# Filling TensorE's planned idle time with matmuls of a constant in an S4 convolution and GEGLU kernel

## The chip, the cores and the metric

The kernel is written for one Trainium2 chip and runs on one core of it. The metric is the device time of one execution in microseconds (us); less is better. A core has a matrix engine (TensorE, PE in the profile, with its weight loads listed as PEld), a vector engine (DVE), a scalar engine (ACT), GpSimd (POOL) and a sync engine (SP) that mostly issues transfers. Each engine works through its own list of instructions in order and waits on semaphores for the others. Matmul results land in PSUM banks.

## What is computed

```python
mod = (_silu(c) @ w_mod).reshape(c.shape[0], 6, 1, -1)
sa, ca, ga, sb, cb, gb = (mod[:, 0], mod[:, 1], mod[:, 2], mod[:, 3], mod[:, 4], mod[:, 5])
h = _layernorm(x, axis=-1) * (1 + ca) + sa
x = x + ga * _A_ref(h, A_A_re, A_A_im, A_B_re, A_B_im, A_C_re, A_C_im, A_log_dt, A_Dskip)
h = _layernorm(x, axis=-1) * (1 + cb) + sb
x = x + gb * _B_ref(h, B_w_gate, B_w_up, B_w_down)
```

x is 2048 tokens by 448 channels. `_A_ref` builds a kernel of 2048 taps for each channel from 256 complex modes, K = Re(sum of C exp(dt A l) dt B), and convolves it with h by FFT. `_B_ref` is (gelu(h w_gate) * (h w_up)) w_down with 1792 inner features.

## The kernel before

The program has two halves. In the first, the S4 half, parameters are turned into exponents and phases (DVE and ACT, function `prep`), written to memory and read back as stationary operands `lt`; TensorE expands them into exponent tables (`exps`, tasks x.mm and y.mm) and phase tables (`angles`); ACT takes exp and sin of them; DVE multiplies (`mults`); TensorE contracts over the modes (`kgen`). Beside it the input is normalised and taken through two stages of a Fourier transform (`u_norm_a`, whose task ua is TensorE's, and `u_stage_b`), then multiplied with the kernel's transform and taken back (`k_fft`, `t_fft`), through memory, into tiles `yi`. The rows of `mod` come from `mod_row`: its task m.mm is four float32 matmuls of silu(c), broadcast as the stationary operand, with 448 columns of w_mod, and its task m.ev is a copy on ACT.

The second half works on four blocks of 512 tokens: `conv_out` ends the inverse transform (task co.mm), adds the residual (DVE), normalises, and transposes on TensorE (co.t in the first block); `gate_up` makes gate and up products in float16 pieces; `down_first` and `down` make the last product.

The order of the work is not written out. Each piece is a task with a cost per engine, dependencies and buffers it takes from pools of fixed size. `Plan.order` simulates the engines with these costs, a due value `v` and tables of leads, picks the next task again and again, and sets `t.start` and `t.end` in its own clock. `Plan.run` then emits the tasks' instructions in that order, and each engine keeps to it on the chip, waiting on semaphores.

Names the text needs: `eps` is a column of 128 rows holding 1e-5 in the tile `small`, set by a memset at L371; `pf`, `pg`, `kg`, `pd` and `pq` are PSUM tiles. Lines: m.mm L768, m.ev L771, ua L832 (its copies out at L408 on ACT and L410 on DVE), y.mm L612, loads of `lt` L575, co.mm L1246 (320 columns) and L1251 (128 columns), the residual add L1257, co.t L1294 and L1296, gate and up L1371 and L1365. In the first block co.mm is split: the first two of its four pieces do the 320 columns (co.mme) and the 128 columns (co.mml) as separate tasks, since the last channels' transform comes back from memory later than the others.

## Time and profile before

| | |
|---|---|
| time, median of 3 runs | 825.76 us (824.82 to 829.9) |
| profiled execution: time | 825.18 us |
| profiled execution: span from first to last instruction | 823.4 us |
| TensorE busy (matmul) | 748.4 us, 91% of the span |
| DVE busy | 599.6 us, 73% |
| ACT busy | 470.3 us, 57% |
| mean granted TensorE clock | 0.969 |

All times of the views are counted from the first instruction of the profiled execution. Its own time is 1.8 us longer than its span. A row of a view gives the start and length, or the busy time, of a group of instructions, its engine and line, the tile written and the tiles read, the shapes, and in square brackets how long the engine had stood idle just before and what ended that. The row PEclk shows the clock that TensorE was granted in tenths of full speed. In the records a float32 matmul appears twice, so a group of four such matmuls is x8.

### The profile page before, as it was taken

What the parts mean: (1) busy time and instruction counts of PE and PEld (TensorE: products, weight loads), DVE (VectorE), ACT (ScalarE), POOL (GpSimd) and SP (SyncE); (2) the same over time, 40 slices, a digit from 0 to 9 for tenths busy, and PEclk for the clock granted to TensorE, in tenths of its full rate; (3) what the DMA queues carried; (4) which work ended last, traced back from release to release, by engine and by line L of the source; (5) the groups of instructions that cost most, each with busy time, mean ns of one, the idle gap of its engine ahead of it and who ended that gap; (6) DMA issues with size and microseconds to landing.
All of it is one profiled execution on the core that took longest, in us unless ns stands there. A gap on an engine that the chain in (4) does not pass through costs nothing.

```text
span 823.4 us, 19059 instructions
## 1 busy us (share of the span) xinstructions
PE 748.4 (91%) x8166; PEld 461.2 (56%) x8166; DVE 599.6 (73%) x981; ACT 470.3 (57%) x629; POOL 6.0 (1%) x14
## 2 busy tenths in 40 slices
PE   2786789999799999998589999999999999999997
PEld 1344344444577767778466445444496445864477
DVE  7789998999889989897494783178863686244542
ACT  5598999899968999971244553034442353113320
POOL 0000000000000000000200000000000000000000
PEclk9888799999999999999889999999999999999999
DMA  9552369996858846899669756245315322022101
GB/s 283 148 167 92 105 189 236 285 273 200 236 146 257 233 133 193 253 307 295 189 197 298 267 179 179 75 140 166 117 53 146 135 91 90 34 79 90 45 12 35
DMA packets 92526, 136.83 MB, mean 166 GB/s; under 512 B 21280, under 2 KB 75200, under 8 KB 92442
## 3 DMA queue, kind: packets, MB, share of 16 engines
q1 hardware_dynamic: 89514, 133.75, 53.8%
q10 hardware_dynamic: 2608, 1.61, 0.8%
q8 instruction: 64, 1.05, 0.5%
q0 software_dynamic: 320, 0.26, 0.1%
q14 instruction: 20, 0.16, 0.1%
HBM read 100.48 MB, written 36.01 MB: 166 GB/s over the span
## 4 chain that ended last, share of the span: by engine, by line
PE 67%; ACT 12%; DVE 10%; DMA 6%; issue 3%; SPq 1%; DVEq 0%; ACTq 0%
PE pq L1371 30%; PE pq L1472 9%; PE pd L1441 3%; PE kg L710 3%; ACT fg L643 2%; PE pg L630 2%; PE pf L999 2%; PE pq L1365 2%; PE pf L768 2%; ACT my L617 2%; PE pf L1085 2%; PE pf L895 2%; DVE tx L679 2%; DMA fg<-in_w_mod 2%; PE pd L1472 1%
## 5 line engine op out<-in xcount | busy, mean ns | idle before, releaser
L1371 PE MATMUL pq<-ht,wr 128*128 128x512 f16 (+1 forms) x1200 | 250.0, 367 | 0.0
L1371 PEld LDWEIGHTS <-wr 128*128 128x128 f16 x1200 | 115.4, 98 | 128.6 <-issue 11.0
L1378 ACT ACTIVATE ge<-pq 128x512 f32<-128x512 f32 (+1 forms) x60 | 33.9, 568 | 144.5 <-PE pq L1365 93.9
L1385 DVE TENSOR_TENSOR fq<-ge,pq 128x512 f32<-128x512 f32 (+1 forms) x60 | 38.5, 649 | 72.1 <-PE pq L1371 48.2
L1397 ACT ACTIVATE hh<-fq 128x1024 f16<-128x1024 f32 (+1 forms) x49 | 47.1, 963 | 54.5 <-DVE fq L1385 41.8
L1472 PE MATMUL pq<-d,hh 128*128 128x224 f16 x504 | 73.2, 259 | 0.0
L710 PE MATMUL kg<-ty,tx 128*32 128x64 f32 x3584 | 61.8, 221 | 11.3 <-DVE ty L687 6.4
L679 DVE TENSOR_TENSOR tx<-mx,fg 128x1024 f32<-128x1024 f32 x56 | 68.0, 1220 | 4.0 <-ACT fg L654 2.2
L683 DVE TENSOR_TENSOR ty<-my,fg 128x1024 f32<-128x1024 f32 x56 | 68.2, 1219 | 3.0 <-PE kg L710 2.8
L710 PEld LDWEIGHTS kg<-ty,tx 128*32 128x32 f32 x3584 | 53.0, 110 | 27.6 <-issue 11.2
L1472 PE MATMUL pq<-d,hlo 128*128 128x224 f16 x252 | 65.3, 259 | 0.0
L1400 DVE TENSOR_TENSOR hlo<-fq,hh 128x1024 f16<-128x1024 f32 (+1 forms) x49 | 53.9, 1104 | 5.3 <-ACT hh L1397 5.0
L643 ACT ACTIVATE fg<-pg 128x1024 f32<-128x1024 f32 x56 | 56.6, 1019 | 1.9 <-issue 1.2
L1472 PEld LDWEIGHTS <-hh 128*128 128x128 f16 x588 | 56.7, 98 | 1.1 <-issue 0.4
L617 ACT ACTIVATE my<-pg 128x1024 f32<-128x1024 f32 x56 | 55.3, 1041 | 3.1 <-PE pg L612 2.9
L999 PE MATMUL pf<-q,fc 128*128 128x160 f32 x264 | 42.9, 313 | 0.3 <-DVE q L989 0.3
L630 PEld LDWEIGHTS <-lt 64*128 64x128 bf16 x336 | 20.7, 95 | 37.4 <-issue 20.7
L999 PEld LDWEIGHTS pf<-q,fc 128*128 128x128 f32 x264 | 37.7, 195 | 6.3 <-issue 3.3
L630 PE MATMUL pg<-ea,lt 64*128 64x512 bf16 x168 | 34.9, 389 | 6.2 <-ACT fg L643 4.4
L687 DVE TENSOR_TENSOR ty<-my,fg 128x512 f32<-128x512 f32 x56 | 38.4, 686 | 0.0
L686 DVE SCALAR_TENSOR_TENSOR ty<-my,fg 128x512 f32<-128x512 f32 x56 | 38.4, 685 | 0.0
L735 PE MATMUL kg<-ak,ke 128*64 128x128 f32 x448 | 32.1, 284 | 6.2 <-DVE ke L730 4.4
(172 smaller groups left out, 1196.3 us busy)
## 6 DMA issues: line engine op xcount, KB each, us to landing
wr<-w_d SPq DMA_DIRECT2D x21, 896.0 KB
fc<-in_k_fc SPq DMA_DIRECT2D x20, 576.0 KB
u_d<-so SPq DMA_DIRECT2D x32, 224.0 KB
w<-in_wgu SPq DMA_DIRECT2D x14, 512.0 KB
ui<-u_d SPq DMA_DIRECT2D x10, 672.0 KB
w_d<-wr SPq DMA_DIRECT2D x7, 896.0 KB
fq<-in_wd SPq DMA_DIRECT2D x14, 448.0 KB
us<-uo SPq DMA_DIRECT2D x22, 240.0 KB
```

The source lines that it names most:

```text
L617: A.activation(yb.tile.rearrange("p a b c -> p (a b c)"), pb.tile, AF.Exp)
L630: T.matmul(pa[:, nh * 512:nh * 512 + 512], w, x, start=(k == 0), stop=(k == 2))
L643: A.activation(fb.tile[:, 0].rearrange("p x (n k) -> p n x k", n=2), pb.tile.rearrange("p (n x k) -> p n x k", n=2, x=2), AF.Sin, scale=TW ...
L679: V.tensor_mul(tx.tile, xb.tile[:, xm, None, :].to_broadcast([128, 2, 512]), fb.tile[:, :, 0])
L683: V.tensor_mul(ty.tile[:, 1], yb.tile, fy()[:, 1, :, None, :].to_broadcast([128, 16, 2, 32]))
L710: T.matmul(kg[32 * g:32 * g + 32, 2 * (s % 2) + q, :64], tx[:, r, nh, 4 * q + g], ty[:, r, nh, 4 * q + g], start=(r == 0 and nh == 0), sto ...
L999: T.matmul(pz.tile[:, e % 32 - sl0], fc.tile[:, i, 1 + t], pp.tile[:, t, i], start=(t == 0 and e != 32), stop=(t == 1 and e != 0))
L1371: T.matmul(pb[k].tile[:, ts], wr.tile[:, 4 * lo + t, k, c0:c0 + 128], ht[:, m, ts], start=f % 2 == 0 and i == 0, stop=f % 2 == 1 and i == 9)
L1385: V.tensor_mul(to if half is None else to[:, half:half + 1], *src)
L1397: A.activation(hg.tile[0][:, cb, c], fq.tile[:, c], AF.Copy)
L1400: V.tensor_sub(hg.tile[1][:, cb, c], fq.tile[:, c], hg.tile[0][:, cb, c])
L1472: T.matmul(bank(k)[:, m], x[:, p, q[0], ts], w[:, p, q[1]], start=new and m == 0 and p == 0 and z == 0, skip_group_check=True, stop=i in ( ...
```

## The change

`Plan.run` now keeps, for tasks on TensorE, how long TensorE stands idle in the planner's own clock ahead of the task (`t.idle`). A new helper `spin` takes the planned idle time less 1.2 us, divides it by 0.4 us for 448 columns (less for narrower ones in proportion), and emits that many matmuls of `eps` with `eps`, both broadcast and float32, into the bank that the task overwrites next. Six kinds of tasks call it: x.mm, kgen, m.mm, ua, co.mm and co.t. The order of the tasks stays what it was.

```diff
     def run(self):
+        free = 0.0
         for t in self.order():
+            if t.on == "PE":
+                t.idle, free = t.start - free, t.start + t.eng["PE"]
             t.fn(t.on) if len(t.eng) > 1 else t.fn()
...
+    def spin(me, dst, w=D):
+        for _ in range(int(max(0.0, me[0].idle - 1.2) / (0.4 * w / D))):
+            T.matmul(dst, eps.to_broadcast([128, 128]), eps.to_broadcast([128, w]), start=True, stop=True)
+
...
+        me = []
+
         def mm():
             pb.tile = fft.tile([128, D], FT, name="pf")
+            spin(me, pb.tile)
             for t in range(4):
...
         t2 = add("m.mm", {"PE": 3.22}, v, mm, [t1, t_si], [pb], [wb])
+        me.append(t2)
...
                 for h in range(2):
                     pbs[h].tile = fft.tile([128, D], FT, name="pf")
+                spin(me, pbs[0].tile)
                 for h in range(2):
...
                     if i == 0:
                         pb.tile = POOLS["pd"].tile([128, D], FT, name="pd")
+                    spin(me, pb.tile[:, c0:c1], c1 - c0)
...
                 pt.tile = POOLS["ps"].tile([128, 4, 128], FT, name="pq")
+                spin(me, pt.tile.rearrange("p k t -> p (k t)")[:, :D])
                 for k in range(3):
```

In x.mm the call stands behind `pb.tile = gen.tile(...)`, in kgen behind the allocation of `kg`; both read like the ones shown.

In the built program the helper gives instructions at four places, 105 matmuls in all, and all are on TensorE: 33 ahead of the first m.mm, 7 ahead of the first ua, 59 of 128 columns ahead of the first co.mml, and 6 ahead of the third co.t. No other engine's list has other instructions than before. In the changed program line numbers are larger: L768 is L784, L832 is L852, L612 is L623, L1246 and L1251 are L1270 and L1275, L1294 and L1296 are L1322 and L1324; the helper's matmul is L417.

TensorE's list at the start of the program, with the semaphores that each row waits for (`fg` holds w_mod, `pk` silu(c), `xt` the normalised input). Before:

```order
L768 MATMUL pf<-fg,pk 128x448 [waits DMAHW6_49,DMAHW1_49,Activation_49]
L768 MATMUL pf<-fg,pk 128x448 x3
L768 MATMUL pf<-fg,pk 128x448 [waits DMAHW7_49]
L768 MATMUL pf<-fg,pk 128x448 x3
L768 MATMUL pf<-fg,pk 128x448 [waits DMAHW0_49,Activation_49]
L768 MATMUL pf<-fg,pk 128x448 x3
L832 MATMUL pf<-xt,au 128x448 [waits DMAHW4_49,DMAHW5_49,DVE_49,Activation_49]
L832 MATMUL pf<-xt,au 128x448 [waits Activation_49]
```

The same place now:

```order
L417 MATMUL pf<-small 128x448 [waits DVE_49]
L417 MATMUL pf<-small 128x448 x32
L784 MATMUL pf<-fg,pk 128x448 [waits DMAHW6_49,DMAHW1_49,Activation_49]
L784 MATMUL pf<-fg,pk 128x448 x3
L784 MATMUL pf<-fg,pk 128x448 [waits DMAHW7_49]
L784 MATMUL pf<-fg,pk 128x448 x3
L784 MATMUL pf<-fg,pk 128x448 [waits DMAHW0_49,Activation_49]
L784 MATMUL pf<-fg,pk 128x448 x3
L417 MATMUL pf<-small 128x448 [waits Activation_49]
L417 MATMUL pf<-small 128x448 x6
L852 MATMUL pf<-xt,au 128x448 [waits DMAHW5_49,DMAHW4_49,DVE_49]
L852 MATMUL pf<-xt,au 128x448 [waits Activation_49]
```

The 33 matmuls wait for DVE alone (the memset of `eps`), and the loads' semaphores are waited for behind them; the 7 take over a wait for an ACT copy that frees their bank.

TensorE's list at the passage from the first half to the second (`yi` is the transform read back, `ai` and `ident` are constants, `xn` is the normalised block). Before:

```order
L1246 MATMUL pd<-yi,ai 64x320 x4
L1251 MATMUL pd<-yi,ai 64x128 x4
L1246 MATMUL pd<-yi,ai 64x320 x2
L1251 MATMUL pd<-yi,ai 64x128 x2
L1246 MATMUL pd<-yi,ai 64x320 x2
L1251 MATMUL pd<-yi,ai 64x128 x2
L1294 MATMUL pq<-ident,xn 128x128 x3
L1296 MATMUL pq<-ident,xn 64x128 x2
L1294 MATMUL pq<-ident,xn 128x128 x3
L1296 MATMUL pq<-ident,xn 64x128 x2
L1294 MATMUL pq<-ident,xn 128x128 x3
L1296 MATMUL pq<-ident,xn 64x128 x2
```

The same place now:

```order
L1270 MATMUL pd<-yi,ai 64x320 x4
L417 MATMUL pd<-small 128x128 x59
L1275 MATMUL pd<-yi,ai 64x128 x4
L1270 MATMUL pd<-yi,ai 64x320 x2
L1275 MATMUL pd<-yi,ai 64x128 x2
L1270 MATMUL pd<-yi,ai 64x320 x2
L1275 MATMUL pd<-yi,ai 64x128 x2
L1322 MATMUL pq<-ident,xn 128x128 x3
L1324 MATMUL pq<-ident,xn 64x128 x2
L1322 MATMUL pq<-ident,xn 128x128 x3
L1324 MATMUL pq<-ident,xn 64x128 x2
L417 MATMUL pq<-small 128x448 x6
```

The 59 stand ahead of the matmuls that read the late part of `yi`, and take over from them a wait for DVE (the residual add that reads the same bank); the 6 stand ahead of the third transpose, and wait for nothing.

## The prediction

> **What bounds the kernel now.** I read the page first, for the shape of the run.

> ```profile
> span 823.4 us, 19059 instructions
> PE   2786789999799999998589999999999999999997
> PEclk9888799999999999999889999999999999999999
> ```

> Each digit is a fortieth of the span, 20.6 us. TensorE is short of work and of clock at the start and around 400 us, and nearly full from there on. The change puts matmuls at just these two places, so I followed the chain of waits through them; first the start.

> ```profile
> 2.63 13.19 DMA fg<-in_w_mod
> 15.96 12.27 PE pf L768 x24
> 28.33 4.86 DMA lt<-lh_d
> 33.24 1.39 PE pg L612 x4
> ...
> 45.44 5.77 DMA xt<-in_A_u
> ```

> The chain runs through m.mm without a gap: a load until 15.82, the twelve matmuls until 28.23, then the load of `lt` and what needs it. Why the load of `lt` hangs on m.mm is seen in ACT's own list, in order of time, where it stands behind the copies of m.mm's results:

> ```profile
> 22.24 0.54 ACT L771 ACTIVATE rows<-pf 128x448 f32<-128x448 f32 x1 [6.01 <-PE pf L768]
> ...
> 28.25 0.54 ACT L771 ACTIVATE gs<-pf 128x448 f32<-128x448 f32 x1 [1.84 <-PE pf L768]
> 28.33 1.38 ACTq L575 DMA_DIRECT2D lt<-lh_d  x2
> ```

> So whatever moves the end of m.mm moves the first half. Now the same chain at the passage to the second half:

> ```profile
> 376.54 4.73 PE pf L1069 x40
> ...
> 389.63 8.95 PE pf L1085 x80
> ...
> 407.64 2.45 DMA yi<-y
> ...
> 410.23 0.91 PE pd L1251 x4
> ...
> 419.50 0.70 DVE xn L1289
> ...
> 420.25 0.94 PE pq L1294 x6
> 421.18 0.43 PE pq L1296 x4
> 421.61 3.85 PE pq L1371 x20
> 425.46 0.32 PE pq L1365 x4
> 425.78 2.29 PE pq L1371 x20
> ```

> A readback of `yi` ends at 410.09, a little TensorE follows, then DVE's residual adds and norms until 420.20, the third transpose, and the gate and up products, which keep TensorE full to the end. Its L1371 rows are the same twenty matmuls, 3.85 us in one and 2.29 in the other.

> **The price of one added matmul.** The planner's idle time is divided by 0.4 us for 448 columns. The trace has no such matmul; the nearest is m.mm's: float32, a broadcast stationary operand, 448 columns moving. Four of them late in the run, and then those of L768 at the start in two stretches (length, TensorE busy, records, weight loads, granted clock, DMA):

> ```profile
> 233.23 3.01 PE pf L768 x8
> ```

> ```profile
> 20.50:22.00 1.50, 1.50 (x3) 0.68 (x2) 1.00 0.42 163
> 22.00:23.50 1.50, 1.50 (x5) 0.76 (x4) 1.00 0.30 93
> ```

> Late in the run a matmul takes 0.752 us (3.01 for four, two records each). At the start they run at half that pace until about 22 us: the clock column reads 1.00 in both rows, but the count of records per 1.5 us says otherwise, and I go by the count. So TensorE needed 6.0 us of work (15.96 to 22) to get its clock. The other stretches of that kind, with the granted clock in the last column but two:

> ```profile
> 33.20:36.60 3.40, 3.36 (x11) 1.59 (x11) 2.10 (x5) 3.25 (x5) 0.00 (x0) 0.50 0.04 16
> ...
> 410.50:413.90 3.40, 3.40 (x20) 2.08 (x20) 2.57 (x9) 0.59 (x2) 0.00 (x0) 0.50 0.95 260
> 413.90:417.50 3.60, 3.28 (x26) 2.12 (x22) 3.46 (x9) 1.20 (x3) 0.00 (x0) 0.91 0.90 356
> 417.50:421.20 3.70, 0.95 (x8) 0.83 (x10) 3.62 (x8) 3.54 (x6) 0.00 (x0) 1.00 0.00 1
> 421.20:424.00 2.80, 2.80 (x16) 1.88 (x17) 2.73 (x6) 1.04 (x1) 0.00 (x0) 0.53 0.51 161
> 424.00:427.00 3.00, 3.00 (x26) 2.17 (x25) 2.96 (x6) 1.29 (x2) 0.00 (x0) 0.87 0.34 139
> ```

> After the wait for `yi` the clock is at half from 410.2 to about 414.5 (0.91 over 3.6 us is 0.65 us at half), 4.3 us; it falls again after the 0.95 busy us of 417.5 to 421.2 and is back at about 424.8 (0.87 over 3.0 us is 0.8 at half), 3.6 us.

> **The start, 33 matmuls.** They wait only for the memset of `eps`:

> ```profile
> 0.81 0.06 DVE L371 MEMSET small<- 128x1 f32 x1 [0.81 <-PEq L1632]
> ```

> They start at about 1.0. 33 x 0.752 is 24.8 us. While the clock is still at half they lose half of that stretch; of stretches between 3.6 and 6.0 us that is 1.8 to 3.0, and I take 2.5. They end at 28.3. m.mm's data landed at 15.82, but m.mm stands behind them in TensorE's list. It then has the full clock, 12 x 0.752 = 9.0 us, and ends at 37.3 where it ended at 28.23: **+9.1 us** (8.4 to 9.6). The gain of the clock, 12.27 - 9.0 = 3.3 us, is in this. Nothing covers the delay: behind the copies of L771 stand, in ACT's list, a store of `lh` and the loads of `lt`, and DVE's norms need the copies. SP's loads are not held by it, but none of them ends the chain here.

> [...]

> **The start, 7 matmuls.** They fill the gap ahead of the first ua, and ACT waited for TensorE a little later:

> ```profile
> 31.48 1.16 PE L832 MATMUL pf<-xt,au 64*128 64x448 f32 x4 [3.26 <-issue]
> ```

> ```profile
> 39.28 3.77 ACT L617 ACTIVATE my<-pg 128x1024 f32<-128x1024 f32 x4 [1.68 <-PE pg L612]
> ```

> 7 x 0.752 = 5.3 us in a gap of 3.26: ua comes 2.0 us later. Behind ua stands y.mm, whose `lt` lands 5.0 us after m.mm (33.24 - 28.23); it now waits for 5.3 and a ua of 0.6, +0.9. In exchange TensorE has its full clock where it had 0.50, and ACT's wait of 1.68 us can go. From 39.28 on ACT is full and TensorE's clock no longer matters. Bounds -1.7 and +2.0; I take **0**, as the two ends weigh about the same.

> **The passage, 59 matmuls of 128 columns.** What waits and for how long, on TensorE, and the add that they wait for, on DVE:

> ```profile
> 398.94 1.30 PE L1246 MATMUL pd<-yi,ai 128*64 128x320 f32 x8
> 410.23 1.32 PE L1251 MATMUL pd<-yi,ai 128*64 128x128 f32 x8 [9.99 <-DMA yi<-y]
> ```

> ```profile
> 399.75 0.49 DVE L1257 TENSOR_TENSOR x<-x,pd 128x320 f32<-128x320 f32 x1 [4.15 <-PE pd L1246]
> ```

> Start 400.24. Nearest rows for 128 x 128 x 128 float32: L1085, 8.95/40 = 0.224 us, and L1069, 4.73/20 = 0.2365; from the wide one by columns, 0.752 x 128/448 = 0.215. 59 take 12.7 to 14.0 us; with the row that has most of them, 13.2. They end at 413.4, the data were there at 410.09: **+3.2 us** (2.7 to 3.8). The clock is kept, so the four records of L1251 on the chain take half of 0.91: -0.45.

> **The passage, 6 matmuls.** The gap they fill:

> ```profile
> 420.25 0.94 PE L1294 MATMUL pq<-ident,xn 128*128 128x128 f32 x6 [3.07 <-DVE xn L1289]
> ```

> 6 x 0.752 = 4.5 us in 3.07: **+1.4** (at half clock 9.0, +5.9, which after 13 us of matmuls I don't expect). The first twenty of L1371 keep the clock: 2.29 for 3.85, **-1.6**. TensorE is the chain from there on, so the rest arrives at the end. Passage together +3.2 - 0.45 + 1.4 - 1.6 = **+2.6** (2.1 to 3.2).

> **Sum.** The profiled execution took 825.18 us (span 823.4 and 1.8 around it). 825.18 + 9.1 + 0 + 2.6 = 836.9; it stands 0.6 below the median of 825.76, so I forecast **837 us**; its own range is 834 to 840.5.

> **Rivals.**

> *The delay of the start is hidden.* The chain shows one way only; if another within a few us set the end of the first half (between 45 and 376 us the chain goes from ACT to DVE to transfers), part of the 9.1 would vanish. It decides from 3 us hidden: below 834 the loss is within 1%. All hidden: 825.2 + 2.6 = 828. For it: the 5.77 us load in the chain may get shorter when it runs at another time. Against: that load is released by TensorE, and ACT and DVE both stand behind L771, in lists whose order is fixed. 0.15.

> *Not slower: the added matmul is as cheap as the planner's 0.4 us.* A moving operand that is one broadcast column is in no row. From half of 0.752 downwards the 33 end by 1.0 + 33 x 0.376 + 2.5 = 15.9, when the data land, the 7 take 2.8 of 3.26 us, the 59 take 6.7 of 9.99, and the 6 take 2.4 of 3.07. Then only the gains are left: -3.3 - 1.7 - 0.45 - 1.6 = -7, 818 us, still within 1%. Against: L768 has the same type, width and broadcast weights and never ran faster. 0.07.

> [...] That is inside this rival, with 0.02 of its 0.07; the trace, at 0.376 us a record, disagrees.

> *The constant does not bring up the clock.* If tiny constants did not count as work, the 33 would take 49.6 us and m.mm its 12.27 as before: +34.6; the 7 some +5, the 59 some 4 us at full and the rest at half clock, +12, the 6 +6: 882 us. Against: m.mm's own work raised the clock with broadcast weights. 0.05.

> *My forecast*, 0.73.

> **Range and chances.** 1% of the median, 8.3 us, is about what a measurement of this kernel can tell from no change: 817.5 to 834. My range is 828 to 841: it takes in the hidden start and leaves out the cheap matmul, the cold constant and a tail of 0.06. Slower: forecast 0.73 less 0.05 below 834, cold 0.05 and 0.01 of the hidden start, 0.74. Faster: 0.02 of the cheap one. Same: 0.24.

> **What would show it.** In the profile after: records of the new line at 0.376 us for 448 columns and 0.112 for 128, the first stretch ending near 28 and the first m.mm right behind it with no idle time; the copy of L771 near 32; the first ua near 42.6; 13 us of the new line at the passage, with L1251's successor following it and the wait for `yi` gone; granted clock near 1.00 through both. I am wrong if m.mm starts before 27, if the distance from the end of m.mm to the end of the first half shrinks by 3 us or more, or if the new records are shorter or stay at 0.75 us.

## The result, and the profile after

The changed kernel takes 834.83 us (median of 6 executions, 832.26 to 840.71); the kernel before took 826.12 us beside it (median of 6, 823.47 to 830.65). The ratio is 1.0104, with a 95% interval of 1.0062 to 1.0146: 8.6 us slower, between 5.1 and 12.1. That is slower by just over 1%, where the forecast was 837 us. The profiled execution of the changed kernel took 836.45 us, 11.3 more than that of before (825.18).

The page of the changed kernel, its slices of 20.9 us:

```profile
span 834.6 us, 19477 instructions
PE   9968687999999999998999999999999999999997
PEclk9999598999999999999999999999999999999999
```

TensorE now reads 9 in the first two slices and in the 20th and 21st (they were 2 and 7, 5 and 8), and the clock is 9 in all four. (In the fifth slice the clock reads 5 where it read 7 before.) The whole gets longer all the same. The chain of waits at the start shows why; its columns are the start, the length and what it was:

```profile
0.92 27.52 PE pf L417 x66
28.44 9.02 PE pf L784 x24
37.47 5.29 PE pf L417 x14
42.75 1.00 PE pf L852 x4
...
55.04 5.45 DMA xt<-in_A_u
...
408.24 0.71 PE pd L1270 x4
409.51 13.44 PE pd L417 x118
422.95 0.42 PE pd L1275 x4
...
429.04 4.73 PE pq L417 x12
433.77 0.67 PE pq L1322 x6
434.81 2.29 PE pq L1400 x20
437.42 2.29 PE pq L1400 x20
```

The 33 added matmuls (66 records of line 417) are now the start of the chain, in place of the load that landed at 15.82. They end at 28.44; m.mm (L784, formerly L768) takes 9.02 us where it took 12.27, and ends at 37.46 where it ended at 28.23. At the passage the 59 end at 422.95, where L1275 (formerly L1251) began at 410.23. The 6 take 4.73 us, and gate and up (L1400, formerly L1371) get both their twenties in 2.29. The second of these twenties began at 425.78 before and begins at 437.42 now, 11.64 later; the rest to the end takes as long as before (397.28 us, 397.69 in before).

ACT's list shows the delay handed on as the prediction read it: the copies of m.mm's results late, and the load of `lt` behind the last of them.

```profile
31.49 0.55 ACT L788 ACTIVATE rows<-pf 128x448 f32<-128x448 f32 x1 [15.75 <-PE pf L784]
...
37.58 1.37 ACTq L582 DMA_DIRECT2D lt<-lh_d  x2
```

That load is issued 9.25 us later than before (28.33).

### The profile page after: what moved, and what is told of

Read it like the earlier page. It is cut to its first block, busy times and chain, and to the rows that moved or that the text cites. A ratio compares the mean times of both kernels' runs of the same rounds, so it can differ in the third digit from the quotient of the medians.

```text
span 834.6 us, 19477 instructions
## 1 busy us (share of the span) xinstructions
PE 791.3 (95%) x8376; PEld 488.0 (58%) x8376; DVE 598.9 (72%) x981; ACT 470.3 (56%) x629; POOL 6.0 (1%) x14
## 3 DMA queue, kind: packets, MB, share of 16 engines
q10 hardware_dynamic: 2608, 1.61, 0.7%
## 4 chain that ended last, share of the span: by engine, by line
PE 70%; ACT 13%; DVE 9%; DMA 4%; issue 3%; SPq 1%; ACTq 0%; DVEq 0%
PE pq L1400 29%; PE pq L1501 9%; PE pf L417 4%; PE pd L1470 4%; ACT fg L654 3%; ACT my L628 2%; PE kg L722 2%; PE pq L1394 2%; PE pf L916 2%; ACT fg L646 2%; PE pf L1106 2%; PE pg L641 2%; DVE ty L694 2%; DVE tx L690 2%; PE pd L417 2%
## 5 line engine op out<-in xcount | busy, mean ns | idle before, releaser
L1400 PE MATMUL pq<-ht,wr 128*128 128x512 f16 (+1 forms) x1200 | 248.5, 365 | 0.0
L1400 PEld LDWEIGHTS <-wr 128*128 128x128 f16 x1200 | 114.5, 98 | 127.9 <-issue 11.0
L641 PEld LDWEIGHTS <-lt 64*128 64x128 bf16 x336 | 20.5, 94 | 40.3 <-issue 23.9
L916 PE MATMUL pf<-ui,fu 128*128 128x448 f32 x66 | 33.7, 606 | 1.6 <-DMA ui<-u_d 1.6
```

The lines of the kernel that those rows point to most:

```text
L641: T.matmul(pa[:, nh * 512:nh * 512 + 512], w, x, start=(k == 0), stop=(k == 2))
L916: T.matmul(pb.tile, fu.tile[:, i], ui.tile[:, EORD[e0 + i] % 32 - s0], start=True, stop=True)
L1400: T.matmul(pb[k].tile[:, ts], wr.tile[:, 4 * lo + t, k, c0:c0 + 128], ht[:, m, ts], start=f % 2 == 0 and i == 0, stop=f % 2 == 1 and i == 9)
```

## The experiments

Mine and three rivals stood at the outset. Mine: the parts add up, +9.1 at the start, 0 for the 7 and +2.6 at the passage, since an added matmul costs 0.752 us and every microsecond ahead of m.mm reaches the end. The rivals of the prediction: the start's delay is partly hidden further on, the matmul is cheaper than that, or the constant does not raise the clock. All edits below are against the changed kernel. The kernel before ran beside each group, with medians of 826.59 to 828.26 us; each difference is worked out from the ratio to it.

**The start alone, and the passage alone.** The first keeps only m.mm's 33, the second only the 59 and the 6:

```diff
-                t.idle, free = t.start - free, t.start + t.eng["PE"]
+                t.idle, free = t.start - free if t.n in ("m.mm",) else 0.0, t.start + t.eng["PE"]
...
+                t.idle, free = t.start - free if t.n in ("co.mml", "co.t") else 0.0, t.start + t.eng["PE"]
```

> Only the 33 matmuls ahead of the first m.mm are left in. Theory 'overrun' (each added matmul takes 0.752 us, nothing hides what goes past the arrival of the data): the 33 end near 28.4 us, m.mm ends near 37.4 instead of 28.2, the first matmul of t.fwd starts at 385.7 instead of 376.5, the wait for yi is back at about 10 us, and the time is 9 us above the kernel before. Rival 'hidden' (another way sets the end of the first half): m.mm ends at 37.4 too, but t.fwd starts within 3 us of 376.5 and the time is within 3 us of the kernel before. Rival 'extra load' (the loss of the changed kernel has nothing to do with this place): no change in time.

> Only the 59 and the 6 matmuls at the passage are left in. Overrun: m.mm ends at 28.2 and t.fwd starts at 376.5 as in the kernel before; the 59 take 13.4 us and end 3.4 us after the data could be used; the second group of twenty L1371 matmuls starts at 428.2 instead of 425.8, and the time is 2.4 us above the kernel before. Rival 'clock pays' (what the clock wins at the passage outweighs the overrun): that group starts at 425.8 or earlier and the time is not above the kernel before.

The start alone took 831.09 us, ratio 1.0039 [1.0005, 1.0074], +3.2 us. The passage alone took 830.54 us, 1.0057 [1.0028, 1.0085], +4.7 us. Neither is what my sum gives (+9.1 and +2.6), although in the profile of the start alone m.mm did exactly what it did in the changed kernel:

```profile
27.72 9.18 PE L784 MATMUL pf<-fg,pk 112*128 112x448 f32 x24
```

It ends at 36.90, 8.7 us later than before, and yet the time is up by 3.2. So either the delay is hidden further on, or something else gained some 5 us. The next runs were chosen for that.

**The planner's price at 0.8 us.** With that price 16 matmuls stand ahead of m.mm, 3 ahead of ua, and 29 and 3 at the passage:

```diff
-        for _ in range(int(max(0.0, me[0].idle - 1.2) / (0.4 * w / D))):
+        for _ in range(int(max(0.0, me[0].idle - 1.2) / (0.8 * w / D))):
```

> The planned idle time is divided by 0.8 us for 448 columns instead of 0.4: 16, 3, 29 and 3 matmuls. Overrun: the 16 end at 15 to 16.5 us, when the data land; m.mm runs at full clock and ends near 25 instead of 28.2 (-3.2); the 29 end by 407, before the data; the third transpose is not delayed and the first twenty of L1371 take 2.3 instead of 3.85 us (-1.5); the time is 4 to 7 us below the kernel before, 819 to 822. Rival 'no help' (the clock that the added matmuls win is worth nothing at the end): the time is within 1 us of the kernel before.

819.36 us, ratio 0.9900 [0.9857, 0.9942]: 8.3 us faster than before, and the lowest time of the study (two others lie within 1.5 us of it). Its 16 fit into the wait for the load (16.32 us against 15.82), and the 29 into the wait for `yi`:

```profile
0.92 15.40 PE pf L417 x32
16.32 9.04 PE pf L784 x24
```

```profile
406.28 1.32 PE L1275 MATMUL pd<-yi,ai 128*64 128x128 f32 x8 [2.90 <-DMA yi<-y]
```

m.mm ends at 25.35 instead of 28.23, which accounts for 2.9 us. The passage is 1.6 us shorter than in the profile of before. That leaves several microseconds unexplained, on the same side as in the start alone.

**Is the delay of the start hidden?** Two kernels with wide matmuls ahead of m.mm alone, 49 of them (price 0.275) and 8 of them (price 1.6), both with the condition on `m.mm`:

```diff
+        for _ in range(int(max(0.0, me[0].idle - 1.2) / (0.275 * w / D))):
...
+        for _ in range(int(max(0.0, me[0].idle - 1.2) / (1.6 * w / D))):
```

> 49 matmuls of 448 columns ahead of the first m.mm, none elsewhere. They end near 40.3 us and m.mm ends near 49.4, 21 us later than in the kernel before and 12 us later than with 33. If every us past the arrival of the data is carried to the end, the time is 12 us above that of the kernel with 33 at this place, 842 to 844. If the start is half hidden by other work, it is 5 to 7 us above it, 836 to 838.

> Only 8 matmuls ahead of the first m.mm. They end near 9.5 us and leave some 6 us idle. If what the added matmuls win is the clock at the moment m.mm starts, the clock has fallen again by then, at least for part of the time: m.mm takes 10.5 to 12.3 us from 15.96 and ends at 26.5 to 28.2. If any early work wins it (a first use of the array, loading of code), m.mm takes 9.0 us and ends at 25.

```profile
0.92 39.30 PE L417 MATMUL pf<-small 128*128 128x448 f32 x98 [0.92 <-DVE small L392]
40.06 9.18 PE L784 MATMUL pf<-fg,pk 112*128 112x448 f32 x24
```

The 49 take 844.93 us, 1.0224 [1.0170, 1.0278], +18.5. m.mm ends at 49.25, 12.35 us after that of the start alone, and the time is 844.93 - 831.09 = 13.8 us longer (15.3 by the two ratios). So what is added ahead of m.mm is carried to the end, all of it: the rival of the hidden start falls. What the start alone had gained must come from elsewhere.

The 8 end at 9.25, a wait of 6.93 us follows, and m.mm takes its old 12.2 us:

```profile
16.18 12.21 PE pf L784 x24
```

Whatever the 8 did to the clock, m.mm shows nothing of it behind that wait: 12.2 us, against 12.27 in before and 9.04 right behind the 16. The single execution took 833.91 us, within the scatter of such singles, so its time decides nothing.

**The same number of instructions, little time.** 33 matmuls of 64 columns ahead of m.mm, in place of 448:

```diff
-            T.matmul(dst, eps.to_broadcast([128, 128]), eps.to_broadcast([128, w]), start=True, stop=True)
+            T.matmul(dst[:, :64], eps.to_broadcast([128, 128]), eps.to_broadcast([128, 64]), start=True, stop=True)
```

> As many matmuls ahead of the first m.mm as in the changed kernel, 33, but of 64 columns, and none elsewhere: the same number of instructions without the delay. They end before 15.8 us; m.mm starts when its data land and ends at 25 to 28.5. Theory 'instruction load' (in the kernel before, TensorE stands idle for 3.4 us at 223.55 in the middle of a kgen task because its next 16 KB of instructions land only then, and the place of that border moves with every instruction added ahead): the idle time is gone, the distance from the end of m.mm to the start of t.fwd is 344 to 347 us instead of 348.3, and the time is 3 to 7 us below the kernel before. Rival 'warm start' (what the changed kernel wins behind the start comes from TensorE's clock right behind its 40 matmuls): the clock falls again before m.mm here, the idle time at 223 stays, the distance is 348 to 352 and the time is within 2 us of the kernel before.

```profile
0.92 14.35 PE L417 MATMUL pf<-small 128*128 128x64 f32 x66 [0.92 <-DVE small L392]
15.06 11.67 PE L784 MATMUL pf<-fg,pk 112*128 112x448 f32 x24
```

820.81 us, 0.9928 [0.9898, 0.9959], -6.0. They end at 15.27, m.mm follows without a wait, and its end moves by only -1.5 us, so the missing microseconds are gained without a delay of the start. The distance from the end of m.mm to the start of t.fwd, the last work of the first half, shrank from 348.33 us to 344.09.

**The trace between 30 and 376 us.** That distance holds stretches in which TensorE does nothing and the trace names no releaser. The longest in before stands in the middle of a run of like matmuls (TensorE's list, in order of time):

```profile
221.67 1.88 PE L710 MATMUL kg<-ty,tx 128*32 128x64 f32 x107
226.93 0.86 PE L710 MATMUL kg<-ty,tx 128*32 128x64 f32 x21 [3.38 <-issue]
```

Its operands were there: the first 107 of the 128 had run on them. The DMA table of the same stretch (224.4 to 225.7) has a row of another kind, with the packets, the megabytes and the share of 16 engines:

```profile
q1 hardware_dynamic: 10, 0.05, 11.4%
q8 instruction: 1, 0.02, 5.2%
```

The page of before gives the busy time and the number of TensorE's records, and the whole of that queue:

```profile
PE 748.4 (91%) x8166; PEld 461.2 (56%) x8166; DVE 599.6 (73%) x981; ACT 470.3 (57%) x629; POOL 6.0 (1%) x14
...
q8 instruction: 64, 1.05, 0.5%
```

The packets support it too. Taken in order, each packet of this queue can be set beside one of these borders. In all 23 breaks over 0.8 us of the fourteen traces TensorE goes on 1.31 to 1.54 us after the end of its packet; in before the packet runs from 224.45 to 225.54, and TensorE is back at 226.93. At the other borders the packet had ended at least 1.0 us before TensorE came to them. By this reading TensorE stood idle for 0.8 to 4.3 us at these 23 borders because its next 16.4 KB of program came late, and instructions added ahead move the borders. The reading from the count was made before the 33 narrow matmuls were run, and their expectation states it; that run and the following ones test it.

**The kernel before once more.** If the place belongs to the program and not to chance, another execution of the same program breaks at the same record.

> The kernel before once more, to see what moves between two executions of one program. The idle time of 3 to 3.5 us in the middle of the kgen task that begins near 222 stands at the same matmul, if it belongs to the instructions' place in their list; the distance from the end of m.mm to the start of t.fwd is 348 to 352 us.

```profile
222.63 1.93 PE L710 MATMUL kg<-ty,tx 128*32 128x64 f32 x107
228.72 0.86 PE L710 MATMUL kg<-ty,tx 128*32 128x64 f32 x21 [4.16 <-issue]
```

It does: behind the same 107th matmul, 4.16 us this time. (This single execution took 831.54 us.)

**128 and 256 added instructions that take almost no time.** A matmul of 32 x 32 in float32 is two matmul records (32 of them are the x64 below) and as many weight loads (8166 of each on the page of before), so 32 are 128 instructions and 64 are 256. The theory of the pieces says that 128 shift the borders by half a piece, and 256 put them back where they were; all other theories expect the two to be alike.

```diff
-        for _ in range(int(max(0.0, me[0].idle - 1.2) / (0.4 * w / D))):
-            T.matmul(dst, eps.to_broadcast([128, 128]), eps.to_broadcast([128, w]), start=True, stop=True)
+        for _ in range(64 if me[0].idle > 4.0 else 0):
+            T.matmul(dst[:32, :32], eps.to_broadcast([128, 32]), eps.to_broadcast([128, 32]), start=True, stop=True)
```

> 64 matmuls of 32 x 32 ahead of the first m.mm and none elsewhere, which end before its data land. A float32 matmul is two loads and two matmuls in the records, so these are 256 instructions, 16 KB of 64 bytes each, and every later border between two loads of instructions falls on the same place in the program as in the kernel before. Theory 'instruction load': the idle time in the kgen task near 223 is back, now at matmul 2771 (2643 + 128); the distance from the end of m.mm to the start of t.fwd is 349 to 354 us; time 824 to 828, within 2 us of the kernel before. Rival 'early work' (any work of TensorE at the start shortens the first half): distance 344 to 347, time 820 to 823.

> The same with 32 of them, 128 instructions: every border is moved by half its distance. Instruction load: no idle time near 223, distance 344 to 347 us, time 820 to 823, 4 to 6 us below the kernel before and below the kernel with 64. Rival 'early work': the same as with 64.

(Both have the condition on `m.mm`; the second has 32 in the first line.) With 256 added instructions the time is 828.05 us, 0.9992 [0.9967, 1.0018]: no change. With 128 it is 821.37 us, 0.9915 [0.9880, 0.9949]: -7.0 us, with half as many matmuls. TensorE's list at the same work, first with 256 and then with 128:

```profile
222.67 0.86 PE L722 MATMUL kg<-ty,tx 128*32 128x64 f32 x43 [0.49 <-DVE ty L698]
226.27 0.53 PE L722 MATMUL kg<-ty,tx 128*32 128x64 f32 x21 [2.75 <-issue]
```

```profile
0.92 3.38 PE L417 MATMUL pf<-small 128*32 128x32 f32 x64 [0.92 <-DVE small L392]
...
224.30 1.10 PE L722 MATMUL kg<-ty,tx 128*32 128x64 f32 x64
225.89 1.10 PE L722 MATMUL kg<-ty,tx 128*32 128x64 f32 x64 [0.49 <-DVE ty L698]
```

With 256 the break stands ahead of the last 21 matmuls of a task, as in before, 256 records further on in the count; with 128 it is gone (one of 1.08 us stands at 137.89). The 128 end at 4.3 us and m.mm ends at 28.15, as in before, so the 7.0 us owe nothing to the clock of m.mm.

**The 7 ahead of ua alone.**

```diff
+                t.idle, free = t.start - free if t.n in ("ua",) else 0.0, t.start + t.eng["PE"]
```

> Only the 7 matmuls ahead of the first ua are left in. The forecast put them at 0, between -1.7 and +2.0: ua starts 2 us later behind m.mm, the clock is full behind them, and ACT's exponentials at 39.3 start at the same distance from m.mm within 1 us. Time 824 to 829. If it is above that, the ua stage itself is on the path; if below, the clock or the moved instruction borders win more than the 2 us.

833.57 us, 1.0065 [1.0031, 1.0099], +5.4 us, where the prediction had 0 between -1.7 and +2.0. The 7 add 28 instructions, and the breaks are there, one of them where before had none (a third, of 1.52 us, stands at 289.40):

```profile
27.43 5.45 PE L417 MATMUL pf<-small 128*128 128x448 f32 x14
224.77 0.28 PE L603 MATMUL pg<-rd,lt 64*128 64x256 bf16 x1 [2.77 <-issue]
232.89 0.75 PE L722 MATMUL kg<-ty,tx 128*32 128x64 f32 x35 [1.30 <-issue]
```

They don't carry all of it. Behind the passage this execution waits for the first block of the down projection, which before did not (groups of TensorE's instructions after 435 us, with the busy time, the mean, and the idle time ahead of them and what ended it):

```profile
L1470 PE MATMUL pd<-d,hh 128*128 128x448 f16 x112 | 31.8, 365 | 2.2 <-ACT d L1586 1.4 <-DVE d L1589 0.8
```

That wait was 0.2 us in the profile of before and 0.0 in that of the changed kernel; it was 1.9 in the passage alone, 2.3 with the 8, and 1.3 in the first of the two kernels that follow. ACT's `d` waits there for a load, `fq<-in_wd` (between 440 and 520 us five waits of 10.7 us in all in the 7 alone, four of 7.0 in before; the last one in the 7 alone is for a load of 8.55 us that landed at 509.57). Why it lands late in these four executions I can't say; how often it does in the executions without a profile, and so how much of +5.4 it is, stays open.

**The clock by itself.** The last two kernels fit all added work into the waits (12 or 10 wide matmuls ahead of m.mm, 39 and 4 at the passage, none ahead of ua) and differ in small ones that bring the number of instructions ahead of m.mm to 128 or 256:

```diff
+                t.idle, free = t.start - free if t.n != "ua" else 0.0, t.start + t.eng["PE"]
...
+        n = int(max(0.0, me[0].idle - 1.2) / (0.6 * w / D))
+        if me[0].n == "m.mm" and n:
+            n = 12
+            for _ in range(20):
+                T.matmul(dst[:32, :32], eps.to_broadcast([128, 32]), eps.to_broadcast([128, 32]), start=True, stop=True)
+        for _ in range(n):
```

> Matmuls that fit their gaps: 20 of 32 x 32 and 12 of 448 columns ahead of the first m.mm, 39 of 128 columns and 4 of 448 at the passage, none ahead of ua. The 32 at the start move the instruction borders of the first half by half their distance, as in the kernel with 32 small ones. If both gains are real and add up: m.mm ends near 25 (-3), the distance to t.fwd is 344 to 347 (-6), the passage from the first co.mm to the twenty-first gate and up matmul takes 25 us where it took 27.5 on average (-2.5): 814 to 818. If the clock is worth nothing: 820 to 823, as with the 32 small ones alone.

> The same with 54 small and 10 wide matmuls at the start, 256 instructions, which leaves the borders of the first half where they are in the kernel before. What is left is what the added matmuls win by the clock alone: m.mm -3, passage -2.5: 820 to 823, 4 to 7 us below the kernel before. If the clock is worth nothing at the end: within 2 us of the kernel before.

(The second has 10 and 54.) With 128 the time is 820.39 us, 0.9911 [0.9875, 0.9946], -7.4 us; with 256 it is 826.30 us, 0.9973 [0.9945, 1.0000], -2.2 us. Both are slower than expected (814 to 818 and 820 to 823). The second adds 256, as the 64 tiny ones did, whose break stood where before has it, so the difference is my estimate of what its matmuls are worth through the clock alone: about 2.2 us, 0.3%, and by the interval between nothing and 4.6. But it warmed the start only in part. Its 10 wide ones end at 13.38, m.mm starts at 15.82, and soon the clock falls (the last column but two of these rows), so that m.mm takes 10.95 us and not 9.0:

```profile
15.80:17.40 1.60, 1.58 (x4) 0.85 (x5) 1.60 (x1) 0.00 (x0) 0.00 (x0) 0.98 0.96 286
17.40:20.90 3.50, 3.50 (x6) 1.69 (x5) 2.69 (x9) 0.21 (x1) 0.00 (x0) 0.52 1.00 313
```

The first kept its clock through m.mm (9.26 us) and the passage (the eight records behind the wait for `yi` take 0.88 us, 1.32 in before), and yet is no better than 32 tiny matmuls without any warming of the passage (-7.0). In the two profiles it ends m.mm 2.9 us earlier and has a passage 2.9 shorter, and loses 4.4 in the other three parts of the table below; whether other executions lose that too is open.

**The marks side by side.** Each row is one profiled execution (us): the instructions added ahead of the end of the first ua and what they leave over a multiple of 256, the end of m.mm, the distance from there to the start of t.fwd, from there to the first matmul of the passage, from there to the second twenty of gate and up, and the rest; together they are the span. The last column is the timed difference to the kernel before.

| kernel | added, over 256s | m.mm ends | to t.fwd | to passage | passage | rest | timed |
|---|---|---|---|---|---|---|---|
| before | 0 | 28.21 | 348.33 | 22.40 | 26.77 | 397.69 | |
| before once more | 0 | 28.48 | 351.80 | 24.20 | 28.00 | 397.27 | |
| passage alone | 0 | 29.91 | 351.28 | 24.27 | 29.19 | 399.44 | +4.7 |
| 64 tiny | 256, 0 | 26.71 | 351.05 | 23.99 | 27.98 | 397.38 | -0.7 |
| fitted, 54 tiny | 256, 0 | 26.77 | 351.51 | 24.33 | 25.93 | 397.86 | -2.2 |
| 7 alone | 28 | 27.60 | 354.61 | 24.13 | 26.43 | 401.51 | +5.4 |
| 8 early | 32 | 28.38 | 352.30 | 22.39 | 29.10 | 399.95 | |
| price 0.8 | 76 | 25.35 | 345.12 | 24.82 | 25.19 | 397.27 | -8.3 |
| 32 tiny | 128 | 28.15 | 345.36 | 22.39 | 28.48 | 397.28 | -7.0 |
| fitted, 20 tiny | 128 | 25.26 | 346.04 | 24.48 | 25.63 | 398.95 | -7.4 |
| 33 narrow | 132 | 26.72 | 344.09 | 24.25 | 28.04 | 397.37 | -6.0 |
| start alone | 132 | 36.90 | 346.02 | 24.14 | 27.97 | 397.28 | +3.2 |
| the change | 160 | 37.47 | 348.30 | 22.40 | 29.19 | 397.28 | +8.6 |
| 49 early | 196 | 49.25 | 347.79 | 22.40 | 26.61 | 397.27 | +18.5 |

The border's share of the distance can be cut out. From the start of the 25th kgen task to the start of the 29th TensorE takes 20.13 to 20.22 us in the six profiles without a break there (price 0.8, 32 tiny, fitted with 20 tiny, 33 narrow, start alone, the change), and 23.82 to 27.03 us in the eight with one. The breaks themselves make 2.15 to 4.31 us of this; in seven of the eight the clock is at half for 3.4 or 6.8 us behind them, and in the six it is not. In before (the clock is the last column but two, TensorE's busy time the second number):

```profile
226.90:230.20 3.30, 3.27 (x30) 3.11 (x31) 2.31 (x3) 0.38 (x1) 0.00 (x0) 0.50 0.02 5
```

The distance to t.fwd goes by the remainder: 348.3 to 351.8 at 0 (mean 350.8), 352.3 and 354.6 at 28 and 32, 344.1 to 348.3 from 76 to 196. It does not go by what the matmuls do or how long they are. With it the parts add up: the start alone has +8.5 (36.90 less 28.35, the mean of the two rows of before) and -4.8 (346.0 less 350.8), +3.7, and was timed at +3.2; the 49 have +20.9 and -3.0, +17.9, timed at +18.5. The passage alone has +1.5 in the passage (29.19 less 27.7, the mean of the nine executions with nothing added there) and 2.2 in the rest, where it waited for `d`: +3.7, timed at +4.7. Distances from single executions are good to some 2 us only; the five at remainder 0 differ by 3.5.

## Why the prediction was right, point by point

**The start, +9.1.** Right in each row: the 33 end at 28.44 (28.3 was forecast), m.mm takes 9.02 (9.0) and ends at 37.46 (37.3), the copy of `rows` starts at 31.49 (near 32). That nothing covers the delay is shown by the 49, which carried 12.35 more us at m.mm to 13.8 in the time (15.3 by the ratios). This stretch of TensorE's list and clock (length, TensorE busy, weight loads, DVE, ACT, GpSimd, granted clock, DMA share, GB/s) shows the constant at work:

```profile
5.00:28.40 23.40, 23.40 (x63) 11.70 (x62) 14.27 (x38) 8.66 (x16) 0.00 (x0) 1.00 0.72 221
...
409.00:423.00 14.00, 13.95 (x124) 13.37 (x122) 4.50 (x8) 2.03 (x2) 2.76 (x5) 1.00 0.59 172
```

63 records in 23.40 us are 0.371 each at a clock of 1.00. So the rival of the cheap matmul falls (it needed half of 0.376 or less). No run shows a faster pace, for which 0.02 of its 0.07 stood: the 98 records of the 49 took 39.30 us, 0.40 each. The rival of the cold constant falls with the last column but two (1.00 in both).

**The 7, taken as 0.** Right for what they do themselves: in the changed kernel they run from 37.47 to 42.75, ua starts there (42.6 was forecast), and ACT's exponentials start at 48.85, 11.38 us behind the end of m.mm, where they started 11.07 behind it before. That is +0.3 us, and ACT's wait of 1.68 us is down to 0.36. With the 7 alone it is the same, 11.37 (m.mm ends at 27.60 there); in the start alone, which has none of them, it is 10.04, so they may cost some 1.3 us of what the row could have been. First the changed kernel, then the 7 alone:

```profile
48.85 3.77 ACT L628 ACTIVATE my<-pg 128x1024 f32<-128x1024 f32 x4 [0.36 <-issue]
```

```profile
38.97 3.77 ACT L628 ACTIVATE my<-pg 128x1024 f32<-128x1024 f32 x4 [0.35 <-issue]
```

Yet by themselves they measured +5.4. Their 28 instructions leave the borders where the longest distance of the table lies, and behind the passage that execution waited 2.2 us more; the step looked only at the gap that they fill.

**The passage, +2.6.** The 59 take 13.44 us (13.2), the 6 take 4.73 (4.5), both twenties 2.29 as forecast. Against the profile of before the passage is 29.19 - 26.77 = 2.4 longer. But before's execution was a short one: the nine executions with nothing added there have 27.7 on average, and against these it is +1.5, the same in the passage alone. The term was some 1 us too large, because what it is set against was read from one execution. On average over the nine, the stretch up to the end of the wait for `yi` is 0.3 us longer than in before, and the work behind it 0.6 longer (14.2 to 17.0 us; 15.5 in before, where the clock was 0.50 for 7.7 us of it, from 410.23 to 414.53 and from 421.36 to 424.77).

**The sum.** 836.9 was set against a profiled execution of 825.18 us, and the profiled execution after took 836.45. The timed +8.6 is 3.1 less than the forecast's +11.7. About 1.1 of this is the passage. The term that the sum lacked is the price of being 160 instructions further on, which none of my steps had: by the table some -2.5 us (348.3 against 350.8), an estimate from single executions. It happened to help here; at 28 or 32 it goes the other way. And it is small only because two larger ones cancel. Between the 25th and the 29th kgen task the changed kernel is 5.0 us shorter than before, since the break is gone (20.22 against 25.26); between the 9th and the 13th it is 5.7 longer (24.17 against 18.49), where TensorE waited 1.70 us for ACT and 1.61 for the load of `ui` and its clock fell (0.53 from 139.4 to 146). Why it fell behind there is open. So the sum was right in the steps that it names, and right to 3 us by luck in the first half that it took as unchanged. For the start alone the same sum was 6 us off.

**What the clock brought.** The runs show little: 2.2 us of 828, 0.3%, with the start warmed in part, and 0.4 us between the 32 tiny matmuls (-7.0) and the fitted ones that also add 128 instructions (-7.4).

## What to carry to other kernels

Here filling the waits with dummy matmuls paid about 2 us of 826 through the clock, and the overrun ahead of m.mm was carried to the end in full (12.35 us more there made the time 13.8 us longer). So the number should come from the measured pace of the same type and width (0.752 us here, not 0.4), and the matmuls should end before the data land. In this kernel, with 16,332 recorded instructions on TensorE, 128 more that took 3.4 us moved the time by 7.0 us and 132 more that fitted the wait by 6.0, so a small edit should be set against the same kernel with the same number of instructions added in another form. Parts that are tried one by one should not be expected to add up: here they gave +3.2, +5.4 and +4.7 alone, and +8.6 together.

## What was not expected of the hardware

- The trace of before has a queue of the kind `instruction`, with 64 packets of some 16.4 KB, which I read as TensorE's program of 16,332 recorded instructions. At 23 borders of the fourteen traces TensorE stood still for 0.8 to 4.3 us. In before one of them is at 223.55 us, with its operands ready, the packet from 224.45 to 225.54 and TensorE back at 226.93; in all 23 breaks it is back 1.31 to 1.54 us after the packet's end. 128 instructions that end by 4.3 us took 7.0 us off the time, and 256 took off 0.7, within the uncertainty. At the other borders no break of over 0.8 us is seen, and their packet had ended at least 1.0 us before TensorE came to them. What makes a packet late was not tried. The break of before follows a time in which the DMA engines are full, but so does its border at 253 us, which costs nothing (columns as above):

```profile
218.00:224.00 6.00, 5.30 (x139) 3.75 (x135) 5.85 (x8) 5.41 (x7) 0.00 (x0) 1.00 0.99 278
...
247.00:253.00 6.00, 5.58 (x122) 4.57 (x122) 5.29 (x7) 5.95 (x8) 0.00 (x0) 1.00 1.04 307
```
- Two executions of the kernel before differ by up to 12 us (820.23 to 832.13 over the 23 of one group). Part of this is in the marks: the distance from t.fwd to the passage was 22.40 in one execution of it and 24.20 in the other, in which TensorE's clock was down at t.fwd (0.50 from 380.30 to 383.00). Another is a transfer on the chain: the load of w_mod ahead of m.mm took 13.19 us in before and 15.06 in the passage alone, whose program is the same up to there. A forecast against one profiled execution carries this with it.
